# A new written order for a sliding-window attention and gMLP kernel: steps of every engine but SP's transfers change places, 41 element passes change engines, 99 instead of 109 matrix steps in halves

## The chip, the core and the metric

The kernel runs on one core of one Trainium2 chip. The metric is the device time of one execution in microseconds (us). Engines are called PE (matrix engine, TensorE), DVE (VectorE), ACT (ScalarE), POOL (GpSimd) and SP (SyncE, which here only issues transfers). PEld is PE's loading of weights, which the profile counts by itself.

## The reference

Eight batches (B = 8) of 8 heads, 576 positions and 64 columns per head pass through an attention in which a position sees itself and the 63 before it, and then through a gated MLP whose gate mixes positions:

```python
scores = scale * np.matmul(q, k.transpose(0, 1, 3, 2))
mask = (rel >= 0) & (rel < window)                 # window = 64
attn = np.exp(scores - max);  attn = attn / (np.sum(attn, axis=-1, keepdims=True) + 1e-09)
x = np.matmul(attn, v)                             # heads side by side: (8, 576, 512)
h = np.maximum(x @ w_in, 0.0)                      # 512 -> 1024
u, v = h[..., :512], h[..., 512:]
v_n = (v - mu) / np.sqrt(var + 1e-06)              # over the 512 columns
v_s = np.einsum('ts,bsd->btd', w_spatial, v_n) + b_spatial[None, :, None]
out = (u * v_s) @ w_out                            # 512 -> 512
```

All inputs and the output are float32; the kernel works in float16 between.

## The kernel before, in words

The work of a batch is cut into small steps with names. A number after the letter is the batch; behind the underscore stands the piece: for attention steps the half of the heads (0, 1) and a second digit for the half of that, `r` for the remaining rows 512 to 575, and for the gMLP steps the block of 128 rows or columns (0 to 3, and 4 for the last 64 rows).

- Loading: `ldq`, `ldk` (line 404) and `ldv` (425) bring a piece of q, k or v in; `cq`, `ck` cast it to float16 and `tq`, `tk` transpose it on DVE (411). `cv`, `sl`, `su`, `s4` cast v and copy it shifted by 64 rows (buffers hv and hs). A helper `cp` writes a cast or copy for any engine: line 296 on ACT, 299 and 302 in pieces on POOL (a cast of q or k in three pieces), 304 otherwise.
- Weights, once: `ldwin`, `cwin` (w_in), `ldwsp`, `cwsp` (w_spatial in five tiles), `W0` to `W4`, which transpose w_spatial on PE (371) and need all five tiles, with `We0` to `We4`, which evict them from PSUM, `ldwo`, `cwo` (w_out), `ldb`, `cb` (the bias).
- Attention of a batch: `S` scores on PE (471; the remainder `S_r` 539), `E` exp on ACT (478), `M` the mask on DVE (481), `Z` row sums on PE (494), `N` and `n` the inverse as exp(-ln) on ACT (521, 523), `P` attention times v on PE (506, remainder 575), `X` normalisation on DVE (514). The result x stands transposed for the next matmuls.
- gMLP of a batch: `V`, the right half of x @ w_in, on PE, `Vr` relu on ACT (640), `Vb` and `Va` mean and variance on DVE (642, 644), `L1` and `L2` the inverse root on ACT (687, 689), `A` the normalisation on DVE (699; result vn); `U`, the left half, on PE, `Ur` relu on ACT (728); `G`, the mixing of positions, on PE, `Ge` the gate times u on DVE (758); `O` the output matmul on PE, `Oe` its eviction on ACT (617), `st` the store. G of a batch needs all five A of that batch and all of We.
- `D0` to `D26` (798) are warm-up matmuls on a scratch tile whose results nobody reads.

V, U, G and O of a batch are some 0.86 to 1.08 us of PE each. Such a step can be issued whole, as one matmul of 128 columns for each of its terms, or in halves, as two of 64 columns (the helper `halves`, lines 585 to 593; the whole form is line 590, the halved one 593).

Nothing schedules this kernel at build time. The function first lists all steps with what each must wait for, and then issues them in the order of a string, `ORDER`, of 1113 words: the step, its engine (PE for whole, PH for halves, DQ for a transfer on SP's queue) and the number of each buffer or PSUM bank that it takes:

```python
    for word in ORDER.split():
        name, eng, *banks = word.split(":")
        out.append((by.pop(name), "PE" if eng == "PH" else eng, [int(x) for x in banks]))
```

Each engine runs its words in the order of the string, strictly one behind the other; an instruction that waits holds up all that stand behind it on its engine. A step also waits until the buffer it takes was released by its former user. There are four single PSUM banks for V, U, G, O, Z, P, W and D (a bank is free again when the eviction has read it) and two pairs for S. Of float32 input buffers there are eight for q, k and weights and four for v, so a transfer can start only when the cast of an earlier one is done. The order interleaves the batches: scores and transposes of batch b+1 stand among the gMLP steps of batches b and b-1.

Of the kernel before, what the change touches and what calls it, by code (L numbers as in the profile page):

```python
# [48 lines left out]
cv1_11:ACT sl1_11:ACT su1_11:POOL P1_00:PE:3 X1_00:DVE:2 Ge0_2:DVE:0 G0_1:PH:2 Ge0_1:DVE:1
ldq3_1:DQ:5 tq2_0:DVE:3 P1_01:PE:0 X1_01:DVE G0_3:PH:3 ck2_1:POOL:1 G0_0:PH:1 n1_11:ACT cq2_1:POOL:3  # L50
P1_10:PE:2 ldv3_11:DQ Ge0_3:DVE:2 n1_10:ACT S2_0:PE:1:0 E2_00:ACT:1 X1_10:DVE:3 P1_11:PE:0 X1_11:DVE
G0_4:PE:3 Ge0_4:DVE:3 M2_00:DVE tk2_1:DVE:0 E2_01:ACT:0 ldv3_12:DQ V1_3:PE:2 Vr1_3:ACT:5 Z1_r:PE:0
cwo01:POOL ldq4_0:DQ:4 ldv3_13:DQ tq2_1:DVE:1 U1_1:PH:3 N1_r:ACT:2 n1_r:ACT Ur1_1:ACT:5 Ge0_0:DVE:4
V1_0:PH:2 cwo10:ACT Z2_00:PE:0 N2_00:ACT:4 Vr1_0:ACT:6 M2_01:DVE V1_1:PH:3 Vr1_1:ACT:7 S2_1:PE:1:0
P1_r:PE:0 X1_r:DVE:1 U1_2:PH:1 E2_11:ACT:3 Vb1_1:DVE:5 cwo11:POOL E2_10:ACT:2 Vb1_0:DVE:0 V1_2:PH:2
Vr1_2:ACT:2 M2_11:DVE U1_0:PH:3 Ur1_2:ACT:2 cwo00:POOL Z2_01:PE:0 N2_01:ACT:1 M2_10:DVE cq3_0:POOL:0
Vb1_3:DVE:2 tq3_0:DVE:4 Ur1_0:ACT:0 V1_4:PE:2 Vr1_4:ACT:1 U1_4:PH:1 ck3_0:POOL:2 Ur1_4:ACT:4
Vb1_4:DVE:4 S2_r:PE:0:1 Va1_0:DVE Z2_10:PE:0 N2_10:ACT:5 E2_r0:ACT:0 E2_r1:ACT Vb1_2:DVE:1 Va1_2:DVE
Va1_3:DVE n2_01:ACT Va1_4:DVE Oe0_4:ACT:0 Va1_1:DVE L11:ACT:1 L21:ACT M2_r:DVE tk3_0:DVE:5
A1_2:DVE:4 A1_0:DVE:5 U1_3:PH:3 O0_0:PH:1 Oe0_0:ACT:0 O0_1:PH:0 Oe0_1:ACT A1_3:DVE:6 cv2_00:POOL:1  # L60
O0_2:PH:2 S3_0:PE:0:1 Oe0_2:ACT:1 Z2_11:PE:1 ldv5_10:DQ:3 Ur1_3:ACT:1 sl2_00:POOL:0 Z2_r:PE:0
A1_1:DVE:7 su2_00:POOL s42_0:POOL cv2_10:POOL:0 ldv3_00:DQ:0 N2_r:ACT:0 n2_00:ACT A1_4:DVE
N2_11:ACT:3 ldq4_1:DQ:6 ldk4_0:DQ:0 G1_3:PH:2 Ge1_3:DVE:5 sl2_10:POOL:1 su2_10:POOL P2_00:PE:3
X2_00:DVE:0 G1_0:PH:0 Ge1_0:DVE:6 n2_10:ACT P2_01:PE:1 X2_01:DVE O0_3:PH:2 G1_4:PH:3 E3_00:ACT:1
M3_00:DVE cq3_1:POOL:1 s42_1:ACT Ge1_4:DVE:7 cq4_0:POOL:3 Oe0_3:ACT st0_1:DQ P2_11:PE:0 n2_11:ACT
n2_r:ACT E3_01:ACT:0 P2_10:PE:1 X2_10:DVE:1 X2_11:DVE tq3_1:DVE:0 cv3_10:POOL:2 M3_01:DVE G1_2:PH:2
V2_0:PH:3 Vr2_0:ACT:4 ck3_1:ACT:0 ldv4_00:DQ:1 ldv3_01:DQ ldv3_02:DQ ldv3_03:DQ sl3_10:POOL:2
su3_10:POOL ldv3_14:DQ st0_4:DQ ldk4_1:DQ:7 P2_r:PE:1 X2_r:DVE:0 G1_1:PH:0 st0_0:DQ Ge1_1:DVE:8
ck4_0:POOL:2 V2_1:PH:3 Vb2_0:DVE:3 cq4_1:POOL:1 V2_3:PH:1 ldv3_04:DQ Vr2_1:ACT:3 Z3_00:PE:0
N3_00:ACT:2 tk3_1:DVE:1 s43_1:POOL Vr2_3:ACT:0 U2_3:PH:3 Ur2_3:ACT:3 Ge1_2:DVE:9 V2_2:PH:0  # L70
ldv4_10:DQ:2 Z3_01:PE:1 tq4_0:DVE:2 N3_01:ACT:4 S3_1:PE:0:1 E3_11:ACT:3 cv3_00:POOL:3 V2_4:PE:3
Vb2_3:DVE:0 sl3_00:POOL:3 E3_10:ACT:2 Vr2_2:ACT:2 ck4_1:POOL:0 Vb2_1:DVE:1 U2_2:PH:2 Ur2_2:ACT:1
Vr2_4:ACT:6 ldq5_1:DQ:1 U2_1:PH:1 su3_00:POOL Ur2_1:ACT:0 S3_r:PE:1:0 E3_r0:ACT:1 Va2_3:DVE
E3_r1:ACT U2_4:PE:0 Ur2_4:ACT:4 Oe1_4:ACT:0 M3_11:DVE ldq5_0:DQ:2 st1_4:DQ tk4_0:DVE:3 s43_0:POOL
U2_0:PE:2 Ur2_0:ACT:5 O1_2:PE:1 Oe1_2:ACT:1 ldv5_00:DQ:0 ldv4_11:DQ ldv4_01:DQ S4_0:PE:1:0
ldv5_01:DQ ldv4_02:DQ cq5_1:POOL:3 M3_10:DVE ldv5_02:DQ cq5_0:POOL:2 ldv4_12:DQ ldk5_0:DQ:5
Vb2_2:DVE:2 Vb2_4:DVE:4 ldv4_03:DQ cv4_00:POOL:1 Va2_2:DVE Va2_4:DVE Va2_1:DVE Z3_10:PE:0
N3_10:ACT:1 tq4_1:DVE:0 sl4_00:POOL:0 O1_0:PH:3 ldv5_03:DQ su4_00:POOL Va2_0:DVE L12:ACT:0 L22:ACT
# [6 lines left out]
M4_01:DVE tq5_1:DVE:4 V3_2:PH:2 Vr3_2:ACT:7 Vb3_2:DVE:5 S4_1:PE:0:1 Vb3_4:DVE:0 E4_11:ACT:0
U3_4:PE:3 Ge2_2:DVE:1 V3_1:PE:1 Ur3_4:ACT:2 st2_4:DQ tq5_0:DVE:5 ldv6_00:DQ:1 M4_00:DVE Vr3_1:ACT:1
E4_10:ACT:3 G2_0:PE:2 M4_10:DVE Ge2_0:DVE:2 V3_3:PE:3 Vr3_3:ACT:6 Va3_4:DVE cv5_00:POOL:3
S4_r:PE:1:0 E4_r0:ACT:0 U3_0:PH:1 Ur3_0:ACT:4 V3_0:PH:0 Vr3_0:ACT:4 E4_r1:ACT ldv5_11:DQ Vb3_0:DVE:2
Z4_00:PE:3 Z4_10:PE:2 N4_10:ACT:0 N4_00:ACT:1 G2_1:PH:1 Z4_01:PE:0 M4_r:DVE N4_01:ACT:2 Va3_2:DVE
Va3_0:DVE U3_2:PH:2 Ur3_2:ACT:3 Vb3_1:DVE:4 Va3_1:DVE Z4_r:PE:3 N4_r:ACT:5 U3_3:PH:0 U3_1:PH:2  # L90
# [758 lines left out]
```

## Time and profile before

| | |
|---|---|
| median of the three runs | 199.06 us (198.86 to 200.04) |
| the profiled execution | 197.47 us, of which 195.7 are the profile's span |
| busy, PE / PEld / DVE / ACT / POOL | 186.3 / 106.8 / 164.1 / 150.0 / 111.3 us |
| TensorE clock granted (mean) | 0.998 |
| DMA queue of the transfers | 72.1% of the 16 engines, 41.91 MB |

Times in the profile count from the start of the trace; the span begins at 1.27 us. A group row of the profile reads: line, engine, operation, output<-input (partitions x elements, type), xcount | busy us, mean ns of one | idle time of the engine before them, and what ended it. A row of the timeline reads: start us, duration us, engine, line, operation, xcount, and in brackets the idle time just before it with what ended it. The chain of work that ended last is followed back from the last instruction; its rows are start, length, and what ran then. "issue" is time in which an engine waited for nothing that the profile shows.

### The profile page before, as it was taken

Reading aid. Unit: us, or ns where it says so; the run is one execution under the profiler, and the core shown is the slowest. Engines: PE = TensorE matmul, PEld = TensorE weight load, DVE = VectorE, ACT = ScalarE, POOL = GpSimd, SP = SyncE. Lnnn points to the kernel's source line nnn. Section 1 sums busy time; section 2 is a strip of 40 time slices with the busy share of each in tenths; the row PEclk is TensorE's granted clock in tenths of the full one; section 3 lists DMA queues with packets and bytes.
Section 4 is the critical chain, followed back from the end, with each engine's and each line's share of the span. In section 5 each row is a group of like instructions: output and inputs, shape, how many; then the busy total and the mean of one; then the engine's idle time right before and its main releaser. Section 6 shows DMA issues by size and latency. Waiting matters only on the chain.

```text
span 195.7 us, 7663 instructions
## 1 busy us (share of the span) xinstructions
PE 186.3 (95%) x3230; PEld 106.8 (55%) x3230; DVE 164.1 (84%) x305; ACT 150.0 (77%) x281; POOL 111.3 (57%) x196
## 2 busy tenths in 40 slices
...
GB/s 210 378 302 183 364 372 225 297 343 384 241 246 301 352 170 275 315 208 300 289 258 220 290 166 180 280 134 51 293 132 155 66 0 113 150 0 2 180 116 191
DMA packets 50277, 42.73 MB, mean 218 GB/s; under 512 B 39361, under 2 KB 39489, under 8 KB 50242
## 3 DMA queue, kind: packets, MB, share of 16 engines
q1 hardware_dynamic: 50018, 41.91, 72.1%
q8 instruction: 25, 0.41, 0.9%
...
## 4 chain that ended last, share of the span: by engine, by line
PE 61%; DVE 14%; DMA 8%; SPq 6%; POOL 5%; issue 2%; ACT 2%; POOLq 0%; DVEq 0%
PE bank L593 38%; PE bank L590 10%; SPq L425 5%; DMA nv<-in_v_dram 3%; PE pair L471 3%; DVE e L481 3%; PE bank L506 3%; DVE kT L411 3%; DMA wi<-in_moe_w_in_dram 3%; DMA nk<-in_k_dram 3%; PE bank L673 3%; DVE vn L699 2%; PE bank L494 2%; POOL hk L299 2%; DVE x L514 1%
## 5 line engine op out<-in xcount | busy, mean ns | idle before, releaser
L478 ACT ACTIVATE e<-pair 128x1024 f16<-128x1024 f32 x32 | 31.5, 1025 | 13.5 <-PE pair L471 13.0
L593 PE MATMUL bank<-wspT,vn 128*64 128x512 f16 (+3 forms) x490 | 35.6, 290 | 0.6 <-DVE vn L699 0.4
L299 POOL CAST hk<-nk 128x384 f16<-128x384 f32 x42 | 22.5, 569 | 17.7 <-DMA nk<-in_k_dram 9.6
L758 DVE TENSOR_TENSOR g<-bank,ru 128x512 f16<-128x512 f32 (+1 forms) x40 | 24.5, 625 | 7.5 <-PE bank L593 4.5
L642 DVE BATCH_NORM_STATS2 st<-vs 128x6 f32<-128x512 f16 (+1 forms) x40 | 26.1, 669 | 4.6 <-ACT vs L640 4.4
L640 ACT ACTIVATE vs<-bank 128x512 f16<-128x512 f32 (+1 forms) x40 | 23.2, 595 | 8.6 <-PE bank L593 6.3
L302 POOL COPY hs<-hv 64x512 f16<-64x512 f16 (+1 forms) x46 | 28.4, 644 | 1.2
L617 ACT COPY ob<-bank 128x512 f32<-128x512 f32 (+1 forms) x39 | 22.1, 589 | 8.4 <-PE bank L590 6.4
L593 PE MATMUL bank<-x,win 128*64 128x512 f16 (+1 forms) x328 | 27.6, 308 | 0.0
L593 PE MATMUL bank<-win,x 128*64 128x512 f16 x208 | 26.2, 380 | 0.2 <-DVE x L514 0.2
L481 DVE TENSOR_TENSOR e<-e,mask 128x1024 f16<-128x1024 f16 x32 | 25.1, 803 | 0.8 <-ACT e L478 0.7
L299 POOL CAST hq<-nq 128x384 f16<-128x384 f32 x39 | 21.3, 583 | 5.9 <-DMA nq<-in_q_dram 3.6
L593 PEld LDWEIGHTS <-vn 128*64 128x64 f16 (+1 forms) x490 | 18.1, 111 | 11.8 <-DVE vn L699 1.4
L728 ACT ACTIVATE ru<-bank 128x512 f32<-128x512 f32 (+1 forms) x40 | 21.6, 555 | 3.3 <-PE bank L593 3.1
L593 PE MATMUL bank<-wout,g 128*64 128x512 f16 x184 | 22.6, 379 | 0.0
L514 DVE TENSOR_TENSOR x<-bank,lz 128x512 f16<-128x512 f32 x32 | 21.0, 681 | 1.4 <-PE bank L506 1.2
L411 DVE STREAM_TRANSPOSE kT<-hk 128x576 f32<-128x576 f32 x16 | 19.9, 1243 | 1.2 <-POOL hk L299 1.2
L521 ACT ACTIVATE lz<-bank 128x512 f32<-128x512 f32 x32 | 18.8, 598 | 2.6 <-PE bank L494 2.5
L699 DVE TENSOR_SCALAR vn<-vs,mv,ln 128x512 f16<-128x512 f16 (+1 forms) x40 | 17.3, 482 | 3.9 <-ACT ln L689 3.9
L302 POOL CAST hv<-nv 128x512 f16<-128x512 f32 x24 | 17.1, 738 | 5.4 <-DMA nv<-in_v_dram 5.0
L523 ACT ACTIVATE lz<-lz 128x512 f32<-128x512 f32 x32 | 19.8, 636 | 0.3
L411 DVE STREAM_TRANSPOSE qT<-hq 128x576 f32<-128x576 f32 x16 | 19.8, 1240 | 0.1
...
## 6 DMA issues: line engine op xcount, KB each, us to landing
...
```

What stands on the lines that cost most here:

```text
L299: nc.gpsimd.tensor_copy(o[:, n:n + 384], i[:, n:n + 384])
L302: nc.gpsimd.tensor_copy(o[:, lo:hi, :, :], i[:, lo:hi, :, :])
L411: d = add(f"t{name}{b}_{g}", ("DVE", 1.09), key, lambda e: nc.vector.transpose(qt.t[:, :].rearrange("p (i j) -> p j i", j=18), h.t[:, :].b ...
L478: ex = add(f"E{b}_{g}{u}", ("ACT", 0.91), key, lambda e, u=u: nc.scalar.activation(e2[u].t[:, :, :], sc[u].t[:, :, :], AF.Exp, bias=0.0, s ...
L481: mins.append(add(f"M{b}_{g}{u}", ("DVE", 0.65), key, lambda e, u=u: nc.vector.tensor_tensor(e2[u].t[:, :, :], e2[u].t[:, :, :], mask[:, : ...
L514: lambda e, u=u, ob=ob, lz=lz: nc.vector.tensor_tensor(x.t[:, u, :], ob.t[:, :], lz.t[:, :], ALU.mult),
L593: nc.tensor.matmul(o[c:c + 64, :], w[:, c:c + 64], x, start=start, stop=stop)
L617: lambda e: (nc.vector.tensor_copy if last else nc.scalar.copy)(view(), m.t[rows, 0:n]),
L640: rl = add(f"Vr{b}_{j}", ("ACT", 0.49), key, lambda e: nc.scalar.activation(vs.t[0:jn, :], m.t[0:jn, :], AF.Relu), deps=[pv], acq=[vs], us ...
L642: s1 = add(f"Vb{b}_{j}", ("DVE", 0.6), key + 0.02, lambda e: nc.vector.bn_stats(st6.t[0:jn, 0:6], vs.t[0:jn, :]), deps=[rl], acq=[st6], us ...
L728: lambda e, m=m, ru=ru, n=n: nc.scalar.activation(ru.t[:, 0:n], m.t[:, 0:n], AF.Relu), deps=[pu], acq=[ru], uses=[m])))
L758: lambda e, m=m, g=g, ru=ru, n=n: nc.vector.tensor_tensor(g.t[:, 0:n], m.t[:, 0:n], ru.t[:, 0:n], ALU.mult),
```

## The change

Only the string changes; the steps, what they wait for and all code stay. The transfers on SP's queue stand in the same order as before. The other steps stand in a new order, 19 places away on average.

- 27 steps that were in halves are whole (G0_1 G0_2 G0_3 G5_3 G5_4 O0_0 O0_1 O0_2 O3_0 O4_1 O6_2 U1_1 U1_2 U4_4 U6_0 U7_1 U7_3 V1_0 V1_1 V1_2 V5_0 V5_1 V5_2 V5_3 V6_0 V6_1 V6_3), 17 that were whole are in halves (G2_0 G3_0 G3_3 O1_2 O2_1 O6_0 U0_1 U0_4 U2_0 U2_4 U3_4 U7_2 V0_0 V0_1 V0_3 V3_1 V3_3).
- 41 casts, copies and evictions change engines:

| from, to | steps |
|---|---|
| DVE to ACT | cq0_0 We1 We2 We3 |
| DVE to POOL | ck0_0 cq1_0 su0_11 cwin111 cwsp0 |
| POOL to ACT | ck0_1 cwin100 cwin101 cwsp2 ck2_0 s41_1 su1_11 cwo01 s42_0 s43_0 cq5_1 cv5_00 sl6_00 cv7_10 |
| POOL to DVE | cq0_1 cv0_00 sl0_00 cwsp4 cv1_01 |
| ACT to POOL | su0_10 cwin001 cwin011 s41_0 su1_01 cv1_11 sl1_11 cwo10 s44_1 s45_0 su6_00 |
| ACT to DVE | We4 sl1_01 |

- Buffer and bank numbers follow the new order.

The diff replaces nearly all lines of the string. Its beginning, up to the first G of batch 0 and the scores of batch 2:

```diff
-D10:PE:0 D23:PE:1 D20:PE:2 D24:PE:3 D4:PE:0 D13:PE:1 D5:PE:2 ldq0_0:DQ:0 cq0_0:DVE:0 D15:PE:3
-tq0_0:DVE:0 D6:PE:0 ldk0_0:DQ:1 ldk0_1:DQ:2 ck0_1:POOL:1 ldq0_1:DQ:3 ldv0_00:DQ:0 D3:PE:1
-ldq1_0:DQ:4 ck0_0:DVE:2 tk0_0:DVE:1 D16:PE:2 tk0_1:DVE:2 D26:PE:3 S0_0:PE:0:1 E0_00:ACT:0
...
-n0_11:ACT n0_00:ACT cwin110:POOL D12:PE:2 ck1_1:POOL:1 P0_00:PE:1 cq1_1:POOL:3 ldwin000:DQ:3
-cwin000:POOL ldwin001:DQ ldwin010:DQ:4 D8:PE:0 N0_10:ACT:3 s40_1:ACT Z0_r:PE:2 N0_r:ACT:4 n0_10:ACT
-P0_01:PE:3 S1_0:PE:0:1 X0_00:DVE:0 X0_01:DVE P0_11:PE:0 cwin111:DVE P0_10:PE:1 D2:PE:2 X0_10:DVE:1
-ldwin011:DQ ldwsp3:DQ:5 ldwsp2:DQ:6 X0_11:DVE E1_01:ACT:0 M1_01:DVE E1_00:ACT:1 n0_r:ACT P0_r:PE:3
-V0_2:PH:2 X0_r:DVE:0 Vr0_2:ACT:0 V0_0:PE:1 Vr0_0:ACT:1 ldwsp1:DQ:7 ldwsp4:DQ:1 Vb0_2:DVE:0
...
-cwsp1:POOL A0_4:DVE Ur0_2:ACT:2 cwsp0:DVE Z1_11:PE:3 ldwo00:DQ:7 ldwo11:DQ A0_0:DVE:0 Ur0_0:ACT:3
-Z1_10:PE:1 A0_1:DVE:1 N1_10:ACT:0 cwsp4:POOL A0_3:DVE:2 W1:PE:2 We1:DVE ldwo01:DQ ldq3_0:DQ:1
-N1_11:ACT:3 E1_r0:ACT:1 E1_r1:ACT W0:PE:0 We0:DVE A0_2:DVE:3 ldv2_00:DQ:0 ldk3_0:DQ:2 ldv2_01:DQ
-cv1_00:POOL:2 sl1_00:DVE:2 W4:PE:1 We4:ACT W3:PE:3 su1_00:POOL ldv2_02:DQ ldv2_03:DQ ldv2_10:DQ:1
-ldv2_11:DQ W2:PE:2 s41_0:ACT We3:DVE U0_3:PE:0 We2:DVE G0_2:PH:1 cv1_01:POOL sl1_01:ACT ck2_0:POOL:0
...
+D6:PE:0 D7:PE:1 ldq0_0:DQ:0 D8:PE:2 D18:PE:3 ldk0_0:DQ:1 ldk0_1:DQ:2 ldq0_1:DQ:3 cq0_0:ACT:0
+tq0_0:DVE:0 D5:PE:0 D22:PE:1 ldv0_00:DQ:0 D25:PE:2 ldq1_0:DQ:4 D11:PE:3 ck0_0:POOL:1 tk0_0:DVE:1
+ck0_1:ACT:2 D12:PE:0 tk0_1:DVE:2 cq1_0:POOL:3 D4:PE:1 S0_0:PE:0:1 D13:PE:2 E0_01:ACT:0 D10:PE:3
...
+ldwin101:DQ tq1_0:DVE:5 D1:PE:0 ldb:DQ:0 ldk1_1:DQ:1 sl0_10:POOL:1 S1_0:PE:1:0 cwin100:ACT
...
+sl0_11:DVE su0_11:POOL cwin110:POOL N0_r:ACT:4 cwin111:POOL ck1_1:POOL:2 E1_00:ACT:1 X0_00:DVE:0
+cwin101:ACT P0_11:PE:3 ldwin011:DQ ldwsp3:DQ:5 ldwsp2:DQ:7 P0_10:PE:1 X0_01:DVE X0_10:DVE:1 n0_r:ACT
+D3:PE:0 cq1_1:POOL:0 X0_11:DVE E1_01:ACT:0 ldwsp1:DQ:6 ldwsp4:DQ:1 ldv1_00:DQ:2 P0_r:PE:2 D19:PE:0
...
+cwsp1:POOL A0_4:DVE cwsp0:POOL W1:PE:0 E1_r0:ACT:1 A0_0:DVE:1 E1_r1:ACT M1_r:DVE cv1_00:POOL:2
+N1_11:ACT:0 ldk2_0:DQ:3 ldv1_10:DQ:3 Ur0_3:ACT:3 W3:PE:1 ldv1_11:DQ ldq2_0:DQ:4 We1:ACT ldv1_12:DQ
+W4:PE:3 ldv1_13:DQ We3:ACT cv1_01:DVE We4:DVE sl1_00:DVE:2 W2:PE:0 ldv1_14:DQ ldk2_1:DQ:5 sl1_01:DVE
+Ur0_2:ACT:4 ldwo10:DQ:0 ldq2_1:DQ:6 W0:PE:1 We0:DVE Z1_r:PE:3 su1_00:POOL ldwo00:DQ:7 We2:ACT
+su1_01:POOL s41_0:POOL cv1_10:POOL:3 sl1_10:POOL:3 N1_r:ACT:2 A0_3:DVE:2 ldwo11:DQ Z1_10:PE:2
+N1_10:ACT:3 A0_2:DVE:3 ldwo01:DQ n1_01:ACT P1_00:PE:0 X1_00:DVE:2 P1_01:PE:1 X1_01:DVE n1_10:ACT
+G0_0:PH:3 Ge0_0:DVE:0 ldq3_0:DQ:1 ldv2_00:DQ:0 G0_4:PE:2 G0_3:PE:0 ldk3_0:DQ:2 Ge0_4:DVE:1
...
```

More of the change, by code (lines that the diff above doesn't have):

```diff
@@ L49 @@
[L49 to L78, printed above, removed]
@@ L85 @@
[L85 to L90, printed above, removed]
@@ new lines @@
+cwin000:POOL Z1_00:PE:3 N1_00:ACT:5 ldv1_01:DQ ldv1_02:DQ V0_0:PH:1 Vr0_0:ACT:2 tq1_1:DVE:1
+cwin010:DVE Vb0_2:DVE:0 cwin001:POOL Vb0_0:DVE:1 n1_00:ACT V0_4:PE:0 V0_1:PH:2 Vr0_4:ACT:3
+Z1_01:PE:3 Vb0_4:DVE:2 N1_01:ACT:1 Vb0_3:DVE:3 S1_1:PE:1:0 cwin011:POOL Va0_4:DVE E1_11:ACT:3
+E1_10:ACT:2 Va0_0:DVE M1_11:DVE Vr0_1:ACT:4 Vb0_1:DVE:4 cwsp3:POOL U0_0:PE:1 Ur0_0:ACT:0 U0_4:PH:0
+cb:POOL cwsp2:ACT ldv1_03:DQ U0_1:PH:3 Ur0_1:ACT:1 Va0_3:DVE U0_2:PE:2 Va0_1:DVE Va0_2:DVE L10:ACT:0
+M1_10:DVE cwsp4:DVE Z1_11:PE:1 S1_r:PE:0:1 Ur0_4:ACT:2 L20:ACT A0_1:DVE:0 ldv1_04:DQ U0_3:PE:3
@@ new lines @@
+A1_0:DVE:5 A1_3:DVE:6 A1_2:DVE:7 A1_4:DVE Ur1_3:ACT:2 cv2_00:POOL:1 sl2_00:POOL:0 su2_00:POOL
+O0_2:PE:1 S2_r:PE:0:1 U1_4:PH:0 E2_r0:ACT:0 E2_r1:ACT M2_r:DVE ldv3_12:DQ ldq4_0:DQ:5 ldv3_13:DQ
+Oe0_2:ACT:1 Ur1_4:ACT:3 n2_00:ACT U1_0:PH:3 Ur1_0:ACT:4 Z2_10:PE:2 N2_10:ACT:1 S3_0:PE:0:1
+Z2_11:PE:1 cv2_10:POOL:0 G1_3:PH:0 N2_11:ACT:3 s42_0:ACT sl2_10:POOL:1 s42_1:ACT Ge1_3:DVE:5
+G1_0:PH:3 Z2_r:PE:2 Ge1_0:DVE:6 N2_r:ACT:0 ldv5_10:DQ:3 ldv3_00:DQ:0 ldq4_1:DQ:6 ldk4_0:DQ:7
+P2_00:PE:1 O0_3:PH:0 n2_01:ACT n2_r:ACT su2_10:POOL cq3_1:POOL:2 Oe0_3:ACT st0_1:DQ ldv4_00:DQ:1
@@ new lines @@
+Vb3_4:DVE:0 Z4_00:PE:2 Vb3_2:DVE:2 ldv6_00:DQ:1 ldv5_11:DQ ldq6_0:DQ:5 ldv6_01:DQ cv5_00:ACT:0
+n4_11:ACT tk5_0:DVE:0 O2_3:PH:3 Vr3_3:ACT:5 Vb3_3:DVE:4 Va3_0:DVE N4_00:ACT:5 ck5_1:POOL:0 n4_00:ACT
+U3_3:PH:1 Ur3_3:ACT:1 Z4_01:PE:0 N4_01:ACT:3 Va3_3:DVE Va3_4:DVE Va3_2:DVE L13:ACT:1 L23:ACT
+A3_3:DVE:4 A3_0:DVE:5 O2_2:PH:2 ldv5_04:DQ ldk6_0:DQ:7 S5_0:PE:0:1 A3_1:DVE:6 Oe2_2:ACT:1 A3_2:DVE:7
+O2_1:PH:1 A3_4:DVE cv4_10:POOL:2 sl4_10:POOL:1 n4_r:ACT s44_1:POOL su4_10:POOL O2_0:PH:0 Oe2_3:ACT
+Oe2_0:ACT:0 P4_00:PE:2 G3_3:PH:3 ck6_0:POOL:1 Z4_10:PE:0 Oe2_1:ACT tk5_1:DVE:1 X4_00:DVE:0
@@ new lines @@
+Ge3_3:DVE:7 ldv6_10:DQ:2 ldv6_02:DQ ldv6_03:DQ G3_0:PH:1 Ge3_0:DVE:5 ldv5_12:DQ ldv6_11:DQ
+ldv6_12:DQ G3_2:PH:2 E5_00:ACT:2 M5_00:DVE ldv5_13:DQ sl5_00:POOL:2 P4_01:PE:3 n4_01:ACT N4_10:ACT:4
+n4_10:ACT G3_1:PH:0 cq6_0:POOL:3 P4_11:PE:1 X4_01:DVE E5_01:ACT:3 Z5_00:PE:3 ldv6_13:DQ ldk6_1:DQ:6
+Ge3_2:DVE:6 P4_10:PE:2 ldv5_14:DQ N5_00:ACT:2 st2_1:DQ ldq6_1:DQ:0 cv5_10:POOL:3 n5_00:ACT
+S5_1:PE:0:1 G3_4:PH:3 E5_11:ACT:0 Ge3_1:DVE:8 s45_0:POOL su5_00:POOL X4_10:DVE:1 X4_11:DVE
+E5_10:ACT:1 V4_2:PH:0 V4_3:PH:2 P4_r:PE:1 ldv7_00:DQ:0 Ge3_4:DVE:9 sl5_10:POOL:3 s45_1:POOL
```

169 lines of the change are left out of this document (90 added, 79 removed).

## The prediction

> **What bounds the kernel now.** I read the page's engine shares first, then the busy time of each engine by stage, then the waits of PE, and last the chain and the single instructions at the places where PE waits.
>
> ```profile
> span 195.7 us, 7663 instructions
> PE 186.3 (95%) x3230; PEld 106.8 (55%) x3230; DVE 164.1 (84%) x305; ACT 150.0 (77%) x281; POOL 111.3 (57%) x196
> PE 61%; DVE 14%; DMA 8%; SPq 6%; POOL 5%; issue 2%; ACT 2%; POOLq 0%; DVEq 0%
> ```
> ```profile
> 1.27:41.00 39.73, 36.76 (x523) 17.95 (x525) 36.16 (x71) 27.20 (x49) 25.52 (x44) 1.00 1.00 301
> 41.00:144.00 103.00, 102.14 (x2083) 62.47 (x2079) 96.60 (x171) 92.81 (x173) 76.43 (x133) 1.00 0.88 252
> 144.00:196.90 52.90, 47.39 (x630) 26.39 (x626) 31.06 (x65) 29.55 (x60) 8.75 (x15) 0.98 0.26 91
> ```
>
> In the second fence a row is a stretch (start:end, length), busy us and count of PE, its loads, DVE, ACT and POOL, then PE's granted clock, the share of the DMA engines and GB/s. Three stages. Up to 41 us the DMA engines are full (1.00): the start goes at the pace of landings, and a good part of PE's 36.76 us is warm-up matmuls that compute nothing. From 41 to 144 us PE is busy for 102.14 of 103.00 us with DVE close behind (96.60). After that PE has little competition. The granted clock is 1.00 nearly throughout, so no stage is paid for by the clock. So only three things can change the time: the amount of PE work, when PE's useful work gets going, and the few places where PE waits.
>
> The places where it waits, from the chain of work that ended last (start, length, what):
>
> ```profile
> 17.96 5.07 DMA wi<-in_moe_w_in_dram
> 24.51 1.87 POOL hk L299 x3
> 26.38 1.82 POOL hq L299 x3
> 28.59 6.42 DMA nv<-in_v_dram
> ...
> 45.95 0.86 PE bank L590 x4
> ...
> 47.05 1.73 PE bank L593 x16
> ...
> 50.32 0.40 issue
> ...
> 58.45 1.18 DVE kT L411
> ...
> 144.67 0.60 ACT vs L640
> ...
> 151.26 0.18 DVE vn L699
> ...
> 191.24 0.59 ACT ob L617
> 191.85 0.42 DVE ob L617
> ```
>
> To count what PE loses after the start I gave every PE step its usual distance to the next one (0.863 us for a V, U or O step, 1.083 for a G, 0.60 for a scores step S, 0.24 for a P, 0.215 for a Z) and subtracted. From P1_10 at 43.75 us to PE's end at 191.2 the lost time is an estimate of 2.7 us, of which 2.0 us lie at four places: 0.57 behind S2_1 (the "issue" row), 0.28 before S3_0 (the kT row: the transpose of batch 3's k ends just as it starts), 0.32 before G3_4, and 0.58 before S7_1, where G5_1 waited for the chain from Vr at 144.67 to the last vn at 151.26. In the first 41 us some 20.5 us are lost or spent on warm-up. The tail behind PE is an ACT and a DVE eviction and a store.
>
> **The change part by part.** *Un-halving* (27 gMLP steps become whole, 17 whole ones become halves, 109 to 99). A halved step issues eight 64-column matmuls where a whole one issues four of 128 columns.
>
> ```profile
> L593 PE MATMUL bank<-win,x 128*64 128x512 f16 x208 | 26.2, 380 | 0.2 <-DVE x L514 0.2
> L593 PEld LDWEIGHTS <-win 128*64 128x64 f16 x328 | 14.0, 111 | 8.1
> L590 PE MATMUL bank<-win,x 128*128 128x512 f16 x24 | 6.0, 380 | 0.0
> L590 PEld LDWEIGHTS <-win 128*128 128x128 f16 x92 | 4.5, 98 | 3.2 <-issue 0.4
> ```
> A matmul's busy time is 26.2/208 = 0.126 us in halves and 6.0/24 = 0.25 whole: 8 x 0.126 is about 4 x 0.25. The chain says the same: 0.86 us for a whole step (x4), 1.73 for two halved ones (x16). So un-halving is worth 0 in PE time; the loads (8 x 111 = 0.89 us against 4 x 98 = 0.39) run beside the matmuls. If that cover were gone, ten steps fewer would give 10 x (0.89 - 0.39) = 5.0 us; as PEld is busy for only 62.47 of the 103 us, I take 0.
>
> What a mixture of forms does cost is the change between them:
>
> ```profile
> 45.79 1.03 PE L590 MATMUL bank<-win,x 128*128 128x512 f16 x4
> 46.75 0.30 PE L562 MATMUL bank<-er,ones 128*64 128x128 f16 x4
> 46.88 1.03 PE L593 MATMUL bank<-x,win 128*64 128x512 f16 x8
> 47.75 1.03 PE L593 MATMUL bank<-win,x 128*64 128x512 f16 x8
> ```
> From the whole step to the 64-column step behind it are 46.75 - 45.79 = 0.96 us, from one halved step to the next 47.75 - 46.88 = 0.87: 0.10 us for a change. Of the changes of form outside the warm-up, by the order of the two kernels, 32 cost this before and 34 after (out of the 32-row scores it is free). +0.2 us, between 0 and +0.4. In the Trainium skill the page TensorEngine Tiling (Array Packing), section Key Properties, says that changing the tiling mode drains TensorE; this trace agrees, at 0.10 us each.
>
> *The start.* Transfers go out in the same order on SP, so a landing changes only where a buffer comes free at another time; I found none that is late. What changes is who casts. DVE loses cq0_0 (to ACT), ck0_0, cq1_0, su0_11, cwin111, cwsp0 (to POOL) and three of the w_spatial evictions, We1, We2, We3 (to ACT); it takes over cq0_1, cv0_00, sl0_00, cwsp4, cv1_01, sl1_01 and We4.
>
> ```profile
> L304 DVE CAST hq<-nq 128x1152 f16<-128x1152 f32 x2 | 1.8, 907 | 1.1 <-DMA nq<-in_q_dram 1.1
> L304 DVE COPY wspT<-bank 128x576 f16<-128x576 f16 x4 | 1.6, 445 | 0.0
> L296 ACT COPY wspT<-bank 64x576 f16<-64x576 f16 x1 | 0.6, 644 | 0.0
> 8.22 1.40 POOL L299 CAST hk<-nk 128x384 f16<-128x384 f32 x3 [5.04 <-DMA nk<-in_k_dram]
> 13.34 2.21 POOL L299 CAST hk<-nk 128x384 f16<-128x384 f32 x3 [2.21 <-DVE qT L411]
> 22.25 0.67 PE L471 MATMUL pair<-qT,kT 32*128 32x128 f16 x56
> 25.29 0.41 PE L593 MATMUL bank<-win,x 128*64 128x512 f16 x2 [0.19 <-DVE x L514]
> 29.49 1.23 DVE L411 STREAM_TRANSPOSE qT<-hq 128x576 f32<-128x576 f32 x1
> 30.78 0.67 PE L471 MATMUL pair<-qT,kT 32*128 32x128 f16 x56 [0.67 <-DVE qT L411]
> 35.34 2.40 PE L371 MATMUL bank<-id,wnat 128*128 128x128 f16 x25
> 36.97 0.64 ACT L296 COPY wspT<-bank 64x576 f16<-64x576 f16 x1
> ```
> With a cast of q or k at 0.91, an eviction We at 0.445 and the rest at an estimated 0.4 to 0.6, DVE gives away some 5.3 us and takes some 3.7: 1.6 us less for it in the first 45 us, where it is the engine that is late. I walked the new order through by hand, each operation by its row, each transfer at its landing of before. The first scores S0_0 have two warm-up steps fewer ahead of them (-0.5 us). S1_0 now stands ahead of the P steps of batch 0 and comes at 19.7 in place of 22.25. cwin101 is cast by ACT as it lands (17.96 + 5.07 = 23.03), not by POOL; the last X of batch 0 ends 1.1 us earlier, and the first V step no longer stalls (the row at 25.29). POOL is then free when k1_1 lands and casts it and q1_1 back to back, so that S1_1 comes at 29.45 in place of 30.78: a lead of 1.3 us. This depends on POOL: by the row at 8.22 a cast of three pieces is 1.40, by that at 13.34 it is 2.21 and by the chain 1.87 and 1.82 for these very ones; at the latter the lead is 0.4.
>
> Then comes W, the transposes of w_spatial (35.34). They wait for the last of its tiles whatever PE's lead. In the old order DVE evicts four of the five and ACT one (36.97); in the new one ACT has We1, We3 and We2, each behind others: E1_r0, E1_r1, N1_11, Ur0_3 stand ahead of the first, Ur0_2 ahead of the last. By the walk ACT is through with We2 at 38.8, and P1_00 waits besides for su1_01, which has gone to POOL (39.3). The lead is used up there: at P1_10 the new order has lost 20.7 us against 20.8. So the start is worth 0; bounds are -1.3 (the whole lead is kept) and +0.7 (POOL casts at 2.21 in front of S1_1).
>
> The Trainium skill, page SBUF — State Buffer, section SBUF: two separate sides, says that DVE and GpSimd share one port pair under an exclusive lock, the second to issue being fully blocked. The 2.21 beside the 1.40 speaks for something of the kind; taken strictly, casts put on POOL would cost DVE their length, and the start would be worth +0.7 or more.
>
> *From 41 us to the end.* The other moves (ck2_0, cq5_1, cv5_00, sl6_00, cv7_10, s42_0, s43_0 from POOL to ACT; s44_1, s45_0, su6_00 back) lie beside PE work. In the first 60 us, though, nothing has room to spare:
>
> ```profile
> 46.00:61.00 15.00, 14.39 (x280) 8.11 (x280) 14.61 (x28) 14.31 (x29) 11.62 (x20) 1.00 1.08 275
> 29.45:38.80 9.35, 8.69 (x139) 4.70 (x138) 9.25 (x23) 9.09 (x20) 7.05 (x10) 1.00 1.03 257
> ```
> In the walk the late places mostly vanish: S2_1, S3_0 and S7_1 have their transposes and vn ready, and 0.7 us of PE's 2.7 remain: -2.0. Against it stands that a walk by row durations does not see DVE being slower than its rows: between 46 and 61 us DVE's operations add up to 13.9 us by their usual distances and took 15.0. Half of these 1.1 us I put on PE, +0.5, and another +0.7 for ACT, which is as full there (14.31 of 15.00), has five passes more in all and evicts PE's banks. So -0.8 for this stage, between -2.0 (the walk) and +1.0 (new waits as large as half the old ones come on top). The tail is the same, 0.
>
> **Sum**: 0 + 0.2 + 0 - 0.8 = -0.6 us. The profiled execution took 197.47 us, of which 195.7 are span; it would take 196.9. The median of the runs is 199.06, 1.59 above, so by the same difference 198.5.
>
> **The rivals.**
> Clearly faster: the start's lead outlives W and the middle is as clean as in the walk. For it: DVE, which is late up to 143 us, owes 1.6 us less. Against it: W and ACT's queue. Time: 199.06 + 0.2 - 1.3 - 2.0 = 196.0, and to be over 1% faster (below 197.1) either of the two with half of the other is enough.
>
> Slower: ACT becomes the late engine at W. The place is its queue from E1_10 (behind S1_1) to We2; the price is one to one, since PE goes in order and has P1 and all G of batch 0 behind it. For it: three evictions of 0.644 us that were 0.445 on DVE, and ACT, which serves the E, N and Ur of the same stretch, was busy for 9.09 of 9.35 us there already. Against it: it has also given away casts there (cwin001, cwin011, sl1_01), and it was busy for only 27.20 of the first 39.73 us, so that passes that come early cost it nothing. If We2 ends 2 us later than 38.8, and the transposes of batch 2 are late behind it so that the middle keeps its 2.7 us: +0.2 + 2.0 + 0.5 = +2.7, 201.8. It decides (+2.0 in all) from We2 at about 40.4 on.
>
> Un-halving pays after all: if whole steps load faster on the path, up to 5.0 us go, 194. In the Trainium skill the page TensorEngine Tiling (Array Packing), section Restrictions, says that column tiling disables the fast weight load. The rows show 98 ns for a load of 128 columns and 111 ns for one of 64, but the distance from step to step is the same (0.86 and 1.73/2); a chance of 0.03.
>
> **How the numbers follow.** About 1% (2 us) is what a measurement of this kernel can tell from no change. My forecast, within 1%: 0.42, its own range 197.1 to 200.6. Clearly faster, by the lead and the middle (0.23) or by un-halving (0.03): 0.26. Slower by over 1%, by ACT at W or by several smaller waits that the walk missed in an order as tight as this: 0.32. The range leaves a tenth on either side: 196.2, just over the faster rival's end, to 202.0, just over the slower one's.
>
> **What would show it.** Right: PE rows fewer by some 66 and distances of 0.86 as before; S1_1 near 29.5, W within 35 to 38, P1_10 near 44; PE idle between 41 and 144 us of 0.3 to 0.9; PE's end 0.5 to 1.5 us before 191.2. Wrong: S1_1 after 30.5 (POOL's casts at over 1.8); We2 after 40; PE waiting for ACT's evictions, or DVE late at the transposes of batch 3 near 59 us. If P1_10 comes at 44 and the end is late all the same, it is the middle that I misjudged.

## The result, and the profile after

The new order takes 198.29 us (median of 20 runs, 196.25 to 200.43) beside 199.14 us for the old one in the same session (198.01 to 200.78, 20 runs). The ratio is 0.9938 with a 95% interval of 0.9911 to 0.9965: 0.6% faster, between 0.7 and 1.8 us. The ratio compares the mean of the runs within 1.5% of their kernel's fastest, which leaves out the four slowest of the new kernel and none of the old one; over all 40 runs the medians differ by 0.85 us, 0.4%. Both lie within the 1% that the prediction called no change, and in its direction; 198.29 is 0.2 us from its 198.5.

The profiled execution of the new kernel took 197.65 us, that of the old one 197.47. The pair of profiles shows no gain at all, then; this is the first thing to explain. First the page of the new kernel (span, busy time of the engines) and its busy time by stage, columns as in the prediction:

```profile
span 195.9 us, 7585 instructions
PE 186.4 (95%) x3197; PEld 105.2 (54%) x3197; DVE 163.3 (83%) x303; ACT 154.9 (79%) x286; POOL 105.1 (54%) x187
```
```profile
1.27:41.00 39.73, 35.91 (x559) 17.95 (x561) 35.08 (x68) 29.70 (x53) 24.67 (x41) 1.00 0.96 295
41.00:144.00 103.00, 102.50 (x1971) 59.12 (x1969) 96.24 (x173) 93.88 (x177) 74.16 (x130) 1.00 0.89 254
144.00:197.00 53.00, 48.03 (x671) 28.13 (x667) 31.66 (x63) 30.86 (x59) 5.68 (x12) 0.97 0.26 91
```

PE's work is what it was (186.4 us against 186.3; 3197 matmul rows against 3230 and as many fewer loads, 66 in all). In the middle stage PE is busy for 102.50 of 103.00 us in place of 102.14: it idles 0.5 us, inside the 0.3 to 0.9 that the prediction gave. ACT has taken 4.9 us more, POOL gave 6.2 away, DVE 0.8.

The start, from the timelines of POOL, DVE, PE and ACT and the rows of SP's issues in the new kernel:

```profile
12.41 2.32 POOL L299 CAST hq<-nq 128x384 f16<-128x384 f32 x3 [4.89 <-DMA nq<-in_q_dram]
12.56 1.81 DVE L481 TENSOR_TENSOR e<-e,mask 128x1024 f16<-128x1024 f16 x2
14.68 2.51 POOL L299 CAST hk<-nk 128x384 f16<-128x384 f32 x3
20.98 0.67 PE L471 MATMUL pair<-qT,kT 32*128 32x128 f16 x56 [1.00 <-DVE qT L411]
25.16 2.40 POOL L299 CAST hk<-nk 128x384 f16<-128x384 f32 x3 [1.52 <-DMA nk<-in_k_dram]
25.60 1.59 DVE L481 TENSOR_TENSOR e<-e,mask 128x1024 f16<-128x1024 f16 x2
27.50 1.40 POOL L299 CAST hq<-nq 128x384 f16<-128x384 f32 x3
27.59 1.26 DVE L411 STREAM_TRANSPOSE kT<-hk 128x576 f32<-128x576 f32 x1
28.94 0.45 SPq L346 DMA_DIRECT2D ws<-in_moe_w_spatial_dram  x1
30.25 0.67 PE L471 MATMUL pair<-qT,kT 32*128 32x128 f16 x56
35.55 0.67 POOL L304 CAST wnat<-ws 128x576 f16<-128x576 f32 x1 [0.76 <-DMA ws<-in_moe_w_spatial_dram]
36.28 2.40 PE L371 MATMUL bank<-id,wnat 128*128 128x128 f16 x25 [0.24 <-POOL wnat L304]
38.40 0.73 ACT L296 COPY wspT<-bank 128x576 f16<-128x576 f16 x1
```

S1_0 comes at 20.98 (walk: 19.7) and S1_1 at 30.25 (walk: 29.45), since three of POOL's casts of q or k took 2.32 to 2.51 us where the walk had 1.40. Each of the three ran beside two masks M on DVE (line 481; two of the pairs are shown); the cast at 27.50, beside a transpose, took the 1.40. W starts at 36.28, not earlier but 0.94 later than before's 35.34. Of this 0.73 us is the last of the five tiles of w_spatial, issued at 28.94 and in the old profile at 28.21 (rows below), because SP stands in order and an earlier transfer waited for a buffer that is cast later now. The other 0.2 us is the change of engine of its cast: 0.67 us on POOL, 0.44 on DVE in the old kernel.

```profile
28.21 0.33 SPq L346 DMA_DIRECT2D ws<-in_moe_w_spatial_dram  x1
34.84 0.44 DVE L304 CAST wnat<-ws 128x576 f16<-128x576 f32 x1
```

ACT is through with We2 at 38.40 + 0.73 = 39.13 (walk: 38.8), so the rival that put the loss in ACT's queue at W (from 40.4 on) did not happen. Counted as in the prediction, the new order has lost 21.4 us at P1_10 in this execution (old: 20.7) and 23.3 at PE's end (old: 23.5). P1_10 itself starts at 45.56, not near 44 as forecast: the new order has some 0.75 us more PE work ahead of it, three changes of form more, and the loss.

In the middle one large wait stands out, from the waits of PE and its timeline: O1_2 for the gate Ge1_2, which DVE runs behind the transpose of batch 4's k.

```profile
PE bank L593 <- DVE g L758: 0.5, 1, 0.5
```
```profile
78.97 0.62 PE L593 MATMUL bank<-wout,g 128*64 128x512 f16 x4 [0.51 <-DVE g L758]
```

The places where the old profile lost (S2_1, S3_0, S7_1) are clean, as forecast. The end of the chain is again PE, an eviction and the store. The eviction starts 0.2 us later than in the old profile; the forecast of a PE end 0.5 to 1.5 us earlier was not met by this pair of executions:

```profile
191.48 0.58 PE bank L782 x8
192.06 0.02 issue
192.08 0.42 DVE ob L617
```

### The profile page after: what moved, and what is told of

Same layout as the page of the kernel before. It is cut to its first block, busy times and chain, and to the rows that moved or that the text cites. A ratio compares the mean times of both kernels' runs of the same rounds, so it can differ in the third digit from the quotient of the medians.

```text
span 195.9 us, 7585 instructions
## 1 busy us (share of the span) xinstructions
PE 186.4 (95%) x3197; PEld 105.2 (54%) x3197; DVE 163.3 (83%) x303; ACT 154.9 (79%) x286; POOL 105.1 (54%) x187
## 4 chain that ended last, share of the span: by engine, by line
PE 74%; DVE 9%; DMA 6%; ACT 4%; POOL 2%; issue 2%; SPq 0%; POOLq 0%
PE bank L593 40%; PE bank L590 19%; DMA nk<-in_k_dram 6%; PE pair L471 4%; PE bank L506 3%; PE bank L494 3%; PE bank L673 3%; ACT e L478 2%; DVE st L642 2%; DVE e L481 1%; DVE qT L411 1%; POOL hk L299 1%; DVE vn L699 1%; DVE kT L411 1%; PE pair L539 1%
## 5 line engine op out<-in xcount | busy, mean ns | idle before, releaser
L593 PE MATMUL bank<-wspT,vn 128*64 128x512 f16 (+3 forms) x440 | 32.9, 296 | 0.1
L640 ACT ACTIVATE vs<-bank 128x512 f16<-128x512 f32 (+1 forms) x40 | 23.3, 596 | 8.2 <-PE bank L593 6.2
L302 POOL COPY hs<-hv 64x512 f16<-64x512 f16 (+1 forms) x46 | 26.7, 607 | 4.5 <-issue 3.3
L299 POOL CAST hq<-nq 128x384 f16<-128x384 f32 x36 | 20.0, 589 | 16.1 <-DMA nq<-in_q_dram 11.4
L593 PE MATMUL bank<-x,win 128*64 128x64 f16 (+1 forms) x376 | 27.1, 286 | 0.0
L728 ACT ACTIVATE ru<-bank 128x512 f32<-128x512 f32 (+1 forms) x40 | 22.3, 565 | 3.0 <-PE bank L593 1.9
L514 DVE TENSOR_TENSOR x<-bank,lz 128x512 f16<-128x512 f32 x32 | 20.7, 681 | 3.0 <-PE bank L506 2.9
L593 PEld LDWEIGHTS <-vn 128*64 128x64 f16 (+1 forms) x440 | 17.0, 111 | 9.9 <-DVE vn L699 0.7
L411 DVE STREAM_TRANSPOSE qT<-hq 128x576 f32<-128x576 f32 x16 | 19.9, 1241 | 2.1 <-ACT hq L296 1.9
L593 PE MATMUL bank<-win,x 128*64 128x512 f16 x168 | 21.6, 380 | 0.0
L411 DVE STREAM_TRANSPOSE kT<-hk 128x576 f32<-128x576 f32 x16 | 19.9, 1243 | 1.7 <-POOL hk L299 0.9
L593 PE MATMUL bank<-wout,g 128*64 128x512 f16 x160 | 20.3, 380 | 0.5 <-DVE g L758 0.5
L523 ACT ACTIVATE lz<-lz 128x512 f32<-128x512 f32 x32 | 19.9, 636 | 0.2
L593 PEld LDWEIGHTS <-win 128*64 128x64 f16 x376 | 14.0, 111 | 8.7 <-issue 0.2
```

The source lines that it names most:

```text
L299: nc.gpsimd.tensor_copy(o[:, n:n + 384], i[:, n:n + 384])
L302: nc.gpsimd.tensor_copy(o[:, lo:hi, :, :], i[:, lo:hi, :, :])
L411: d = add(f"t{name}{b}_{g}", ("DVE", 1.09), key, lambda e: nc.vector.transpose(qt.t[:, :].rearrange("p (i j) -> p j i", j=18), h.t[:, :].b ...
L593: nc.tensor.matmul(o[c:c + 64, :], w[:, c:c + 64], x, start=start, stop=stop)
L640: rl = add(f"Vr{b}_{j}", ("ACT", 0.49), key, lambda e: nc.scalar.activation(vs.t[0:jn, :], m.t[0:jn, :], AF.Relu), deps=[pv], acq=[vs], us ...
L728: lambda e, m=m, ru=ru, n=n: nc.scalar.activation(ru.t[:, 0:n], m.t[:, 0:n], AF.Relu), deps=[pu], acq=[ru], uses=[m])))
```

## The experiments

Lost time below is always PE's time minus its work, step by step, as in the prediction. Line numbers of the kernels made for the experiments are a few higher than those above, since the string takes more lines.

**Parts of the change alone.** *halves* is the old order with only the forms of the 44 steps changed:

```diff
-V0_0:PE:1 ... V1_0:PH:2 ... U1_1:PH:3
+V0_0:PH:1 ... V1_0:PE:2 ... U1_1:PE:3
```

> The old order and engines, only the whole/halved form of the 44 matrix steps as in the new kernel. Un-halving worth nothing (the prediction): ratio to before 1.000, 0.998 to 1.002, PE distances of 0.86 us in both forms. Rival, un-halving is what pays: 0.994 or less.

Measured: 203.2 us, ratio 1.0166 (1.0117 to 1.0216). Both theories were wrong. I had counted the changes of form for the two real kernels only; for this mixture the count gives 67 in place of 31. 36 more at 0.10 us are 3.6 us, and 1.66% of 199.5 is 3.3. From PE's timeline of this kernel, a halved step, a P of batch 6, a whole step and the next P:

```profile
145.00 1.03 PE L595 MATMUL bank<-wout,g 128*64 128x512 f16 x8
145.87 0.22 PE L508 MATMUL bank<-e,hv 128*64 128x128 f16 x2
...
146.21 1.04 PE L592 MATMUL bank<-wout,g 128*128 128x512 f16 x4
147.18 0.25 PE L508 MATMUL bank<-e,hv 128*64 128x128 f16 x2
```

The halved step is followed after 0.87 us, the P in front of the whole step after 0.34 (usually 0.24), the whole one after 0.97. A whole step among 64-column ones pays 0.10 on the way in and 0.10 on the way out; by itself it is neither faster nor slower. Only the steps of block 4 differ, whose matmuls have 64 columns to move: by the distances in the traces U_4 takes 0.47 us whole and 0.50 in halves, G_4 0.60 and 0.63. Two of them became whole and three halved, some 0.04 us together. The 44 changes of form are no gain of their own: they fit the new order.

*engines* is the old order with only the 41 passes moved:

```diff
-cq0_0:DVE:0 ... cwin101:POOL ... We1:DVE
+cq0_0:ACT:0 ... cwin101:ACT ... We1:ACT
```

> The old order and forms, only the engines of the 41 casts, copies and evictions as in the new kernel. Theory, the gain is in the new order behind the start: 1.000 to 1.010, since a pass moved without its place in the order waits behind others. Rival, relieving DVE and the choice of engines is the gain: 0.994 or less.

Measured: 206.33 us, ratio 1.0322 (1.0266 to 1.0379). The rival is out, and the loss is larger than I had allowed for. The chain shows the larger part of it: ACT's cast of win, waiting for its transfer, stands in front of the inverse of the row sums, for which the P steps of batch 0 wait.

```profile
18.46 4.10 DMA wi<-in_moe_w_in_dram
22.58 0.62 ACT win L298
23.20 0.53 ACT lz L525
23.73 0.49 ACT lz L523
24.27 0.64 PE bank L508 x14
```

The first P starts at 24.27 us, in the old profile at 20.33: some 4 of the 6.5 us. The rest was not followed. In the new kernel the inverses of these steps stand ahead of that cast. So neither the forms nor the engines are a gain without the order.

**Which stretch has the gain.** Four kernels join one order up to a step and the other from there on:

```diff
 ORDER = the words of one kernel up to P1_11 (or S3_0), then
+the words of the other that are not yet there, in its order, engines and forms
```

*start* and *rest* are cut at P1_11 (some 45 us), *first60* and *last* at S3_0 (60 us), where only 8 steps stand on the other side of the cut.

> The new kernel's order, engines and forms up to P1_11 of batch 1, then the old order for all that is left. Theory, the start gives nothing (its lead is lost at the transposes of w_spatial, whose last tile lands 0.87 us later in the new profile): 1.000 to 1.004, PE about 0.5 us later at P1_10. Rival, the gain comes from the start: 0.994.

Measured: ratio 0.9955 (0.9915 to 0.9996); the medians of the runs, 199.48 and 199.81 us, differ by 0.2%. The theory's 1.000 lies just outside the interval and the rival's 0.994 inside it.

> The old kernel up to P1_11, then the new order, engines and forms. Theory, the middle gives the gain: 0.990 to 0.995, with less waiting of PE between 46 and 178 us than before's 2.7 us. Rival, the gain comes from the start: 1.000.

Measured: ratio 1.0040 (1.0003 to 1.0077), which misses the theory's 0.990 to 0.995. In its profiled execution the granted clock fell at W, so that profile is not used for the start.

> The new kernel up to S3_0 of batch 3 (60 us in both profiles, only 8 steps stand on the other side of that cut), then the old one. By the profiles so far the starts lose the same (20.8 to 21.8 us against 21.0 to 21.4 at P1_10) and between 41 and 60 us the new order loses 0.6 us less: ratio to before 0.995 to 0.999. Rival, all of the gain is in the start: 0.994; none of it is there: 1.000.

Measured: ratio 1.0069 (1.0032 to 1.0105), slower than all that was expected.

> The old kernel up to S3_0, then the new one. By the profiles so far the new order loses 1.7 to 3.1 us behind 60 us, the old one 1.7 to 5.0 (3.4 in the middle): some 0.9 us less, ratio to before 0.993 to 0.997. Rival, the gain is in the start: 1.000.

Measured: ratio 1.0011 (0.9975 to 1.0047), the rival's 1.000 and not the theory's 0.993 to 0.997.

The parts do not add up to the whole, 0.9938, for first60 and last; for start and rest the intervals are too wide to say. By these times alone the rival that the gain comes from the start is not excluded, and no join with a new end is faster than the old kernel. One clear reason for the misfit is the seam. From the timeline of first60 just behind its cut:

```profile
61.35 0.30 PE L564 MATMUL bank<-er,ones 128*64 128x128 f16 x4 [0.44 <-DVE er L555]
62.07 1.27 PE L595 MATMUL bank<-wspT,vn 128*64 128x512 f16 x10 [0.42 <-ACT lz L523]
```

Counted by steps 1.25 us are lost here, 0.6%, which neither real kernel loses (old 0.1, new nothing at these steps). Without it first60 would be at about 1.001. What a joined kernel measures is the two parts and the joint, and here the joint is as large as the effect. The joints of the other three were not measured.

**What the other profiles say.** Their traces are more use than their times, since they repeat long unchanged stretches. Lost time up to P1_10 (start), from there to S3_0, and from S3_0 to PE's end, in us, of the executions that run that stretch in the order and with the engines of one of the two kernels (the forms of some steps may differ, each change of form counted at 0.10; the other kernels come below; halves, with its 36 changes more, is left out):

| stretch | old order | new order |
|---|---|---|
| start | 20.7 (before), 21.7 (before_best), 21.2 (last) | 21.4 (after), 21.0 (start), 21.3 (after_best), 21.4 (first60), 20.9 (tuned), 19.9 (pool_busy) |
| P1_10 to S3_0 | 1.1 (before), 1.4 (before_best), 1.4 (last), 0.5 (before_late) | 0.1 (after), 0.5 (after_best), 0.1 (first60), 1.2 (tuned), 0.5 (pool_busy), 0.2 (after_late) |
| S3_0 to the end | 1.7 (before), 3.8 (before_best), 3.1 (start), 3.6 (before_late), 4.4 with its seam (first60) | 1.8 (after), 3.2 (after_best), 2.6 (tuned), 3.0 (last), 2.9 (after_late), 2.7 (rest) |

The old profile, on which the prediction was built, is the exception in its row: 1.7 us lost behind S3_0 where its fellows lost 3.1 and more. That is also why it took 197.47 us where the runs had a median of 199.1.

**Forms chosen to change least.** *after_best* halves 28 more steps of the new order, *before_best* 21 of the old one:

```diff
-U0_0:PE:1 ... V1_0:PE:2 ... O7_3:PE:1
+U0_0:PH:1 ... V1_0:PH:2 ... O7_3:PH:1
```

> The new kernel's order and engines, but the form of 28 whole steps halved, so that changes of form outside the warm-up fall from 32 to 23 or so. Theory, a change costs 0.10 us and the forms are worth nothing else: 0.9 us less than the new kernel, ratio to before 0.990. Rival, whole steps are faster for their cheaper loads: no faster than the new kernel, 0.994 or more.

Measured: 198.37 us, ratio 0.9927 (0.9894 to 0.9960), not told apart from the new kernel.

> The old kernel's order and engines with 21 whole steps halved, so that changes of form fall by 8. Theory, 0.10 us each: 0.7 us less, ratio 0.9965. Rival, whole steps are the faster form: 1.000 or more. Its start up to P1_11 is the old one but for forms, so its profile also shows how much the old start loses in another execution: theory, more than the 20.8 us of the first profile, since the old order meets several landings within 0.3 us.

Measured: ratio 1.0002 (0.9968 to 1.0037). 0.7 to 0.9 us less work is not seen in the time: the interval of before_best ends just above the expected 0.9965, that of after_best still holds the expected 0.990. The traces lose elsewhere what the forms save. The second half of the expectation holds: 21.7 us at P1_10 in place of 20.7. Its page and its middle stage also show what differs from one execution of the same order to the next:

```profile
PE 186.3 (94%) x3362; PEld 110.3 (56%) x3362; DVE 167.7 (85%) x305; ACT 150.3 (76%) x281; POOL 111.9 (56%) x196
```
```profile
41.00:144.00 103.00, 100.94 (x2006) 62.38 (x2003) 96.82 (x166) 90.29 (x168) 77.25 (x133) 1.00 0.86 245
```

The same 305 DVE instructions took 167.7 us here and 164.1 in the first profile, and PE idled 2.1 us of the middle stage, not 0.9. Four of DVE's kinds have the same mean in all profiles (gate 0.68, statistics 0.67, x 0.68, transposes 1.24 us); the two that read float16 and write float16 do not: the mask M has 0.803 us on average in the first profile and 0.836 here, the normalisation A 0.474 and 0.541.

**Does POOL slow them?** *pool_busy* gives POOL copies that nobody needs, at A of batches 5 and 7, where it idles in the new order:

```diff
+        if b in (5, 7):
+            def emit_px(e):
+                nc.gpsimd.tensor_copy(tiny[:, :], ln.t[:, 5:10])
+                for _ in range(6):
+                    nc.gpsimd.tensor_copy(scratch[64:128, :], scratch[0:64, :])
```

> The new kernel with seven more POOL instructions at the normalisations A of batch 5 and of batch 7 (a copy of the five scale factors, then six copies of 64x512 from the warm-up scratch to itself, which nobody reads), at places where POOL is idle. Theory, DVE's float16 passes M and A run slower while POOL copies, and that is why the middle varies: the five A of batch 5 go from 1.96 to 2.8 us or more, those of batch 7 from 2.05 likewise, and those of the other batches stay. Rival, A varies for another reason: both stay at 2.0.

The DVE rows of the five A of batch 7, first in the new kernel, then here, with POOL's copies beside them:

```profile
180.24 1.70 DVE L699 TENSOR_SCALAR vn<-vs,mv,ln 128x512 f16<-128x512 f16 x5 [0.61 <-ACT ln L689]
```
```profile
181.12 3.09 DVE L708 TENSOR_SCALAR vn<-vs,mv,ln 128x512 f16<-128x512 f16 x5 [0.67 <-ACT ln L692]
```
```profile
181.47 3.93 POOL L698 COPY scratch<-scratch 64x512 f16<-64x512 f16 x6
```

From 1.70 to 3.09 us for the row; the durations of the single A add up to 2.05 and 3.40 for batch 7, 1.96 and 2.91 for batch 5, and 2.70 and 2.65 for batch 6, which was left alone. The theory holds for the durations: while POOL copies, the A take 1.5 (batch 5) to 1.8 times (the row of batch 7) as long. The time was 199.08 us, ratio 1.0001 (0.9964 to 1.0038) against the new kernel's 0.9938, so about 1 us more, but the two intervals touch. In its trace G5_4 waited 0.87 us behind V6_0 for the A of batch 5; another wait of 0.76 us, of G1_0 near 61 us, stands where nothing was added. How often they meet depends on when each transfer lands, and so differs from run to run. The orders differ in it too: in the new one the five A of batch 2 take 1.88 to 1.91 us (2.36 in this last kernel, though nothing was added there) and those of batch 5 1.92 to 1.96, in the old one 2.10 to 2.89 and 2.61 to 2.96; POOL's casts stand elsewhere. Batch 6 has it the other way, 2.57 to 2.72 us in the new order and 2.00 to 2.13 in the old, and the A of all eight batches add up to much the same: 19.3 to 21.9 us in four executions of the old order (before, before_best, halves, before_late), 19.4 to 21.0 in four of the new one (after, after_best, tuned, after_late). The mask differs more clearly, 0.80 to 0.85 us on average in the former four and 0.77 to 0.80 in the latter, some 1 us of DVE over 32 of them.

**How tight are the landings?** *before_late* and *after_late* issue the transfer of q0_1 twice, into the same tile:

```diff
+                for _ in range(2 if (name, b, g) == ("q", 0, 1) else 1):
                     nc.sync.dma_start(
```

> The old kernel with the transfer of q0_1 issued twice, 576 KB more in front of everything that lands after it, about 1.5 us of transfer time. Theory, the old start meets landings with no slack: nearly all of it is lost, ratio 1.006 to 1.008. Rival, the start is not bound by landings: 1.000 to 1.003.

> The new kernel with the same doubled transfer. Theory, the new start has more slack behind the landings and loses less than the old one: 0.4 us or more less, ratio to before 0.996 to 0.999. Rival, both starts are bound alike: the new kernel's 0.994 plus what the old one loses, 1.000 to 1.002.

Measured: 204.27 us, ratio 1.0233 (1.0192 to 1.0274), and 202.25 us, ratio 1.0135 (1.0084 to 1.0185). Both theories put it far too low: 4.6 us for the old order, and by the ratios (1.0135 - 0.9938) 3.9 for the new one. The difference of 0.7 us is in the direction of the theory, but the intervals are too wide to show it.

The edit did more than add 576 KB, and the 1.5 us of both theories do not describe it. The chain of before_late up to the cast of q0_1:

```profile
2.19 7.13 DMA nq<-in_q_dram
9.32 0.02 issue
9.34 5.07 DMA nq<-in_q_dram
14.41 0.05 issue
14.46 1.43 POOL hq L301 x3
```

The second copy is issued only at 9.34, when the first has landed, and SP, which stands in order, holds all transfers behind it till then: the first of v goes out at 9.71, in the old profile at 2.67. The cast of q0_1 starts at 14.46 in place of 9.72 there. PE in the start of before_late:

```profile
17.23 1.04 PE L476 MATMUL pair<-qT,kT 32*128 32x128 f16 x56 [5.74 <-DVE qT L416]
```
```profile
1.27:41.00 39.73, 32.95 (x467) 15.78 (x468) 30.88 (x60) 23.24 (x41) 20.60 (x37) 0.91 0.92 283
```

S0_1 waited 5.74 us for its q and then ran at 1.04 us in place of 0.67; the granted clock of the stretch is 0.91 (before: 1.00). So 4.7 us later data cost the old order 4.6 us. In after_late the same cast starts at 14.85 us in place of 10.68, 4.2 later, for a cost of 3.9. A late landing in the start is paid for about one to one in both orders; that is what the pair of kernels shows, not what 576 KB more on the queue would cost.

**A version made of the findings.** *tuned* is after_best with one change of places, so that O1_2 finds its gate done:

```diff
-tk4_0:DVE:3 Z3_00:PE:1 G1_2:PH:0 N3_00:ACT:4 Ge1_2:DVE:9
+Z3_00:PE:1 G1_2:PH:0 N3_00:ACT:4 Ge1_2:DVE:9 tk4_0:DVE:3
```

> The new kernel with the forms of after_best, and with the gate Ge1_2 ahead of the transpose tk4_0 on DVE, where O1_2 waited 0.6 to 0.8 us in three profiles of the new order. Theory: that wait goes, 0.5 us less than after_best, ratio to before 0.990. Rival, tk4_0 and with it S4_0 becomes late instead: 0.993 as after_best.

Measured: 198.0 us, ratio 0.9923 (0.9885 to 0.9960). The wait is gone (O1_2 runs in one piece, the row below), but the time is not told apart from after_best (0.9927) or the new kernel (0.9938), and its interval holds both the theory's 0.990 and the rival's 0.993; it is the lowest ratio seen, and faster than the old kernel.

```profile
78.38 1.03 PE L595 MATMUL bank<-wout,g 128*64 128x512 f16 x8
```

## Why the prediction was right, step by step

*Un-halving, 0, and +0.2 for changes of form.* Right: distances stay 0.86 us in both forms, and halves shows the price of a change, 0.09 us measured (3.3 us for 36). What the prediction did not say is that the un-halving would be worth a loss of 3.3 us without the order around it. The rival of faster loads, worth up to 5.0 us, is refuted: the distances are the same but for block 4 (0.03 us a step), and after_best, with 28 more steps in the slower-loading form, lost nothing.

*The start, 0.* Right in the sum (the old order lost 21.2 us on average of three executions, the new one 21.0 of six), wrong in its working. The lead at S1_1 was 0.5 us, not 1.3, because three of POOL's casts took 2.3 to 2.5 us beside M; POOL's casts had been named as the bound, at 2.21. But "I found none that is late" of the transfers was wrong: the last tile of w_spatial was issued 0.7 us later, and its cast on POOL added 0.2. The lead is not used up by ACT's evictions, as the prediction had it; W itself begins late.

*From 41 us to the end, -0.8.* The direction is right, the size rests on one execution. The pair of profiles gives -0.8 (1.9 us lost in place of 2.7). Over the executions in the table, leaving out the value with a seam, the old order loses 1.1 us on average up to S3_0 and 3.0 behind it, the new one 0.4 and 2.7: -1.0. The rows of the two orders overlap, so this is a rough figure, and it does not show by itself in which of the two stretches the gain is. The walk's -2.0 was too much; the losses at the four places that it took away add up to 1.75 us, not to 2.0, and it knew no collisions. The +0.5 and +0.7 that I set against it come near what was needed, but not for the reasons given: no wait of PE for ACT stands in the new profile, so ACT's five passes more were not felt.

*The sum.* -1.0, -0.2 for the start and +0.2 for the forms make -1.0 us; the ratio says -1.2 (-1.8 to -0.7), the medians of all runs -0.85. The forecast of -0.6 was somewhat low. That it came so near is partly luck: the profiled execution of before lies at the lower end of its runs, with 2.7 us lost behind P1_10 where the old order's averages in the table make 4.1, so the walk removed waits of an execution that lost unusually little, and its allowance for collisions happened to balance that.

*What stays open.* Where the gain lies is not shown: the traces put it behind P1_10, while of the joined kernels only start, with the new order up to P1_11, is faster than the old one. Why the joined kernels do not add up is explained only for first60. That the gain in the middle comes from fewer meetings of POOL with DVE's float16 passes is a guess: the shorter M and pool_busy speak for it, but the A of all batches together are no shorter. It was not isolated, since moving the POOL casts alone moves everything behind them. That the new start meets late landings better was not shown.
